# Units of 512 tokens in place of 256 in the feed-forward stage behind the recurrence

## The chip, the cores and the metric

The kernel runs on one core of a Trainium2 chip. The metric is the time of one execution on the device in microseconds (us), the median of several runs. Engines: PE multiplies matrices (PEld is its weight load), DVE, ACT and POOL work elementwise, SP issues the DMAs.

## The reference

A recurrence over 768 steps for 4 x 8 heads of 40 channels makes 3072 tokens of 320 values; two feed-forward layers with 1536 hidden units follow.

```python
for t in range(S):
    y[:, :, t] = einsum('bhd,bhde->bhe', rt, state)
    Sa = einsum('bhde,bhe->bhd', state, at)
    state = state * wt[:, :, None, :] - einsum('bhd,bhe->bhde', Sa, bt) + einsum('bhd,bhe->bhde', vt, kt)
x = y.transpose(0, 2, 1, 3).reshape(B * S, H * D)          # 3072 x 320
g = x @ w_gate;  x = (g * sigmoid(g) * (x @ w_val)) @ w_out      # layer 1
x = (sigmoid(x @ w_gate2) * (x @ w_val2)) @ w_out2               # layer 2
```

## The kernel before, in words

The recurrence works in 12 blocks of 64 time steps, which are 256 tokens each. Beside it the kernel already runs part of layer 1: block m's tokens become a tile x, which goes to memory (xd) too, and as many of the twelve slices of 128 hidden units as are loaded by then (w1) are applied to it. `used[m]` keeps that number: few slices for the early blocks, 11 for the last. The partial sums go to memory (xs[1]) by way of the tile "ob", which has one buffer (L1028, L1029).

Values are kept as float32r in a high and a low part, so a product takes several matmuls. One unit is one block with one slice: `gate` (L771) makes 8 matmuls of 256 columns into a gate bank and 8 into a value bank (L799); ACT takes the sigmoid (L803), DVE multiplies by the gate in layer 1 alone (L805) and by the value (L806), ACT rounds the high part (hh, L807), POOL makes the low part (hl, L808); `add` (L811) then makes 3 matmuls of 320 columns for each 128 tokens (L817) into the output banks.

From the end of the recurrence on, `stream` (L833) runs a list of jobs, one per block: in layer 1 the slices that the block still lacks, in layer 2 all twelve. A unit's output matmuls are issued after the gate matmuls of the next unit. `each` hooks run beside a unit: in layer 1 they load the part sums (L1075) and advance the preparation of layer 2's weights w2 by one step (`load_w`, L678: 36 steps, three a slice, 2 of 384 columns and 1 of 320, with four DVE instructions L701, L702, L706, L707 in each); in layer 2 they reduce w for a check of its range (L1101, L1105, L1106), whose result decides at the end whether a slow path runs. At a block's end its sums are added to the parts and stored (L1085, L1086), or in layer 2 copied and sent to the output (L1093, L1094). Layer 1 fetches x from xd (L1058); layer 2 reads xs[1] and splits it (L734). The framework's scheduler fixes the order on each engine at compile time and may bring loads and preparations forward.

Memory: pools lie on a stack. m_x (one x of 7168 bytes a partition) and m_h (g, hh, hl of 1024 bytes in two buffers each, ob of 1280) are opened first and serve both stages; then m_wa (w1[0] to w1[2]) and at_static; then, in the recurrence, at_work; when it is closed the new stage opens m_wb, m_y (part 2560, xin 3072, wt 1280, two buffers each), m_xq and m_tmp in at_work's place. Eight banks of PSUM: in the recurrence tp (2), zy, qu, pg, mm and two output banks; then two for transposes, two gate, two value and two output banks.

Of the kernel before, what the change touches and what calls it, by code (L numbers as in the profile page):

```python
# [18 lines left out]
P = 128  # L19
# [5 lines left out]
NWB = 2  # L25
# [644 lines left out]
class Ffn:  # L670
# [63 lines left out]
    def split_steps(self, xs):  # L734

        nc = self.nc
        x = self.new_x()
# [24 lines left out]
        yield x  # L762
# [5 lines left out]
    def sums(self, tag):  # L768
        return [self.po.tile([P, DM], F32, tag=f"{tag}{u}", name=f"{tag}{u}") for u in range(2)]

    def gate(self, x, w, silu):  # L771
# [3 lines left out]
        xh, xl = (x[:, 512 * i : 512 * i + 512].rearrange("p (k t) -> p k t", k=2) for i in range(2))  # L775
        t5 = x[:, 1024:1280]
        hd = x[:, 1536:], x[:, 1280:1536]
        if self.one_bank:
            pool, tag = self.pg[self.turn % len(self.pg)]
            gv = pool.tile([P, 2, 256], F32, tag=tag, name="gv")  # L780
            gv = [gv[:, 0], gv[:, 1]]
        else:
            gv = [self.pg.tile([P, 256], F32, tag=f"g{n}", name=f"g{n}") for n in range(2)]
        self.turn += 1
        for n in range(2):
            h = lambda k: wh[:, (3 * n + k) * P : (3 * n + k + 1) * P]
            l = lambda k: wl[:, (2 * n + k) * P : (2 * n + k + 1) * P]
            seq = [
                (h(0), xh[:, 0]),
                (h(1), xh[:, 1]),  # L790
                (l(0), xh[:, 0]),
                (l(1), xh[:, 1]),
                (h(2), t5),
                (h(0), xl[:, 0]),
                (h(1), xl[:, 1]),
                (wl[:, 4 * P : 5 * P], hd[n]),
            ]
            for e, (p, q) in enumerate(seq):
                nc.tensor.matmul(gv[n], lhsT=p, rhs=q, start=e == 0, stop=e == len(seq) - 1)  # L799
        g = self.h.tile([P, 256], F32, tag="g", name="g")  # L800
        hh = self.h.tile([P, 256], F32R, tag="hh", name="hh")
        hl = self.h.tile([P, 256], F32R, tag="hl", name="hl")
# [6 lines left out]
        return hh, hl  # L809
# [11 lines left out]
    def ffn(self, x, ws, silu, tag):  # L821

        ops, pend = self.sums(tag), None
        for f, w in enumerate(ws):
            h = self.gate(x, w, silu)
# [7 lines left out]
    def stream(self, jobs):  # L833
# [6 lines left out]
        for j, (ws, silu, tag, _, each, end) in enumerate(jobs):  # L840
# [3 lines left out]
            ops = self.sums(tag)  # L844
            for f, w in enumerate(ws):
# [11 lines left out]
                if f >= len(ws) - 4 and (nx := next(get, None)) is not None:  # L857
                    get = iter((nx,))
# [117 lines left out]
def rwkv_moe_kernel(ctx, tc, r, k, v, w, a, b, aw0, aw, aa, akb, av, avt, art, w1a, w2a, out):  # L976
# [11 lines left out]
    with ExitStack() as c1:  # L988
        pool = lambda n, b, **kw: c1.enter_context(tc.tile_pool(name=n, bufs=b, **kw))
        x_p, h_p = pool("m_x", 1), pool("m_h", 2)  # L990
# [6 lines left out]
        with ExitStack() as c2:  # L997
            pool2 = lambda n, b: c2.enter_context(tc.tile_pool(name=n, bufs=b, space=PSUM))
# [38 lines left out]
        with ExitStack() as c2:  # L1037
            pool2 = lambda n, b, **kw: c2.enter_context(tc.tile_pool(name=n, bufs=b, **kw))
            wb = pool2("m_wb", NWB)
            y_p, x_q = pool2("m_y", 2), pool2("m_xq", 1)  # L1040
            pt, pg, po = pool2("b_tp", 2, space=PSUM), pool2("b_pg", 2, space=PSUM), pool2("b_po", 1, space=PSUM)
# [4 lines left out]
            slots = [(wb, "w8")] * NWB + [(st, t) for t in spare_tags] + first + [(st, t) for t in tags]  # L1046
# [8 lines left out]
            def load_x(blk):  # L1055
                ffn.x = (x_q, x_p)[blk % 2]
                x = ffn.new_x()
                nc.sync.dma_start(out=x.bitcast(F32), in_=xd[blk])  # L1058
                yield x

            def split_x(blk):
                xin = y_p.tile([P, 2, DM + 64], F32, tag="xin", name="xin")
                src = xs[1][2 * blk : 2 * blk + 2].rearrange("u p e -> p u e")
                nc.sync.dma_start(out=xin[:, :, 0:DM], in_=src)
                nc.sync.dma_start(out=xin[:, :, DM:], in_=src[:, :, 256:DM])
                yield
                ffn.x = (x_q, x_p)[blk % 2]
                yield from ffn.split_steps([xin[:, 0], xin[:, 1]])
# [3 lines left out]
            def each1(blk, f):  # L1072
                if f == 0:
                    part = parts[blk] = y_p.tile([P, 2, DM], F32, tag="part", name="part")
                    nc.sync.dma_start(out=part, in_=xs[1][2 * blk : 2 * blk + 2].rearrange("u p e -> p u e"))  # L1075
                if 1 <= f <= 3:
                    next(ahead, None)
                if blk == NB - 1 and f == NF - 1 - used[blk]:
                    for _ in ahead:
                        pass  # L1080

            def end1(blk, ops):
                part = parts.pop(blk)
                for u in range(2):
                    nc.vector.tensor_tensor(out=part[:, u], in0=ops[u], in1=part[:, u], op=ALU.add)  # L1085
                    nc.sync.dma_start(out=xs[1][2 * blk + u], in_=part[:, u])  # L1086
# [3 lines left out]
            def end2(blk, ops):  # L1090
                ob = y_p.tile([P, 2, DM], F32, tag="part", name="ob")
                for u in range(2):
                    (nc.scalar.copy, nc.vector.tensor_copy)[u](out=ob[:, u], in_=ops[u])  # L1093
                    nc.sync.dma_start(out=out_rows(out, 2 * blk + u), in_=ob[:, u])  # L1094

            def check(blk, f):

                if f in (2, 6, 10):
                    if (n := 3 * blk + f // 4) < 2 * NB:
# [7 lines left out]
                if blk != NB - 2 or f != 8:  # L1107
# [15 lines left out]
            for blk in range(NB):  # L1123
                jobs.append((w1[used[blk] :], True, "po", load_x(blk), partial(each1, blk), partial(end1, blk)))
            for blk in range(NB):
                jobs.append((w2, False, "po", split_x(blk), partial(check, blk), partial(end2, blk)))
# [54 lines left out]
```

## Time and profile before

| what | value |
|---|---|
| median of 3 runs | 1341.2 us (1338.21 to 1343.47) |
| the profiled execution | 1342.04 us, span 1340.3 us |
| mean granted clock of PE | 0.93 |
| PE busy | 1228.5 us, 92% of the span |
| DVE, POOL, ACT busy | 798.8, 599.5, 584.6 us |

Busy shares are means over stages: the recurrence takes the first 690 us, the rest of layer 1 runs to about 920, layer 2 to the end. PE's matmuls are pipelined, so one of 283 ns can follow the other after less; distances between starts tell the pace.

### The profile page before, as it was taken

How to read it: one execution, taken by the hardware profiler on the slowest of the kernel's cores; microseconds unless marked ns; L12 is line 12 of the kernel's file. 1: busy time of each engine (PE TensorE's matmuls, PEld its weight loads, DVE VectorE, ACT ScalarE, POOL GpSimd, SP SyncE). 2: the span in 40 equal slices, each digit the busy share in tenths (PEclk: the TensorE clock that was granted, in tenths of full speed). 3: DMA queues.
4: the chain of work that ended last, by engine and by line, in shares of the span. 5: the costliest groups of instructions: out<-in, count | busy, mean ns of one | idle time of the engine just before them, and what ended most of it. 6: DMA issues, size and time to landing. Idle time of an engine off the chain costs nothing.

```text
span 1340.3 us, 32630 instructions
## 1 busy us (share of the span) xinstructions
PE 1228.5 (92%) x13197; PEld 1166.4 (87%) x13197; DVE 798.8 (60%) x1600; ACT 584.6 (44%) x1416; POOL 599.5 (45%) x798
## 2 busy tenths in 40 slices
PE   4556788799999999999899999999999999999996
PEld 4445777698899888888889999999999999999996
DVE  9778897976687677866879888833112221122111
ACT  5345446456655565545443444423333333333331
POOL 4278586432323322446766888722222222222221
PEclk7565689699999999989999999999999999999998
DMA  6733848645533454143356454221000000000000
GB/s 194 184 101 90 190 139 183 164 110 139 144 114 83 122 143 103 54 123 115 118 185 191 161 163 153 94 70 66 22 23 22 22 23 23 22 23 23 11 11 14
DMA packets 177202, 131.91 MB, mean 98 GB/s; under 512 B 123409, under 2 KB 155153, under 8 KB 176657
## 3 DMA queue, kind: packets, MB, share of 16 engines
q1 hardware_dynamic: 177040, 129.72, 34.8%
q8 instruction: 106, 1.74, 0.5%
q14 instruction: 56, 0.45, 0.1%
HBM read 96.14 MB, written 33.55 MB: 97 GB/s over the span
## 4 chain that ended last, share of the span: by engine, by line
PE 69%; DVE 16%; DMA 4%; issue 3%; ACT 3%; POOL 2%; SPq 2%; DVEq 0%; ACTq 0%; POOLq 0%
PE g L799 28%; PE po L817 16%; PE gv L799 7%; PE tp L312 3%; PE yps L586 3%; PE aps L560 3%; DVE pr L419 3%; PE kps L372 2%; DVE dt L702 2%; DVE part L425 2%; DVE dt L701 1%; PE ups L514 1%; PE qps L496 1%; DVE ds L706 1%; DVE ds L707 1%
## 5 line engine op out<-in xcount | busy, mean ns | idle before, releaser
L799 PE MATMUL g<-x,w 128*128 128x256 f32 x3552 | 494.8, 283 | 4.9 <-issue 3.0
L799 PEld LDWEIGHTS g<-x,w 128*128 128x128 f32 x3552 | 464.3, 190 | 6.3 <-issue 3.3
L808 POOL TENSOR_TENSOR hl<-g,hh 128x256 fp32r<-128x256 f32 x288 | 220.0, 765 | 474.0 <-ACT hh L807 418.7
L806 DVE TENSOR_TENSOR g<-g,g 128x256 f32<-128x256 f32 x222 | 93.8, 423 | 310.5 <-PE g L799 302.4
L807 ACT CAST hh<-g 128x256 fp32r<-128x256 f32 x288 | 117.0, 406 | 261.8 <-DVE g L806 239.2
L817 PE MATMUL po<-w,hh 128*128 128x320 f32 x1152 | 224.3, 311 | 2.3 <-ACT hh L807 1.8
L817 PEld LDWEIGHTS po<-w,hh 128*128 128x128 f32 x1152 | 175.5, 189 | 3.8 <-ACT hh L807 2.6
L799 PE MATMUL gv<-x,w 128*128 128x256 f32 x1056 | 153.8, 296 | 7.4 <-ACT x L751 5.5
L799 PEld LDWEIGHTS gv<-x,w 128*128 128x128 f32 x1056 | 137.1, 196 | 13.5 <-ACT x L751 8.2
L803 ACT ACTIVATE g<-g 128x256 f32<-128x256 f32 x222 | 84.8, 384 | 134.7 <-PE g L799 119.8
L817 PE MATMUL po<-w,hl 128*128 128x320 f32 x576 | 141.3, 316 | 0.6 <-POOL hl L808 0.6
L719 POOL TENSOR_TENSOR dt<-dt,w 128x384 f32<-128x384 f32 (+1 forms) x72 | 79.9, 1110 | 75.2 <-ACT w L717 42.1
L419 DVE TENSOR_TENSOR pr<-part,sn 128x4 f32<-128x4 f32 (+4 forms) x180 | 111.3, 619 | 3.7
L817 PEld LDWEIGHTS po<-w,hl 128*128 128x128 f32 x576 | 91.8, 190 | 2.7 <-POOL hl L808 1.8
L425 DVE TENSOR_REDUCE part<-pr 128x2 f32<-128x4 f32 (+4 forms) x180 | 88.8, 494 | 4.2
L372 PE MATMUL kps<-lq,kbt 104*128 104x128 f32 x384 | 65.6, 324 | 20.2 <-DVE lq L384 17.4
L372 PEld LDWEIGHTS kps<-lq,kbt 104*128 104x128 f32 x384 | 57.6, 229 | 24.7 <-issue 16.0
L384 DVE TENSOR_TENSOR lq<-kps,part 64x256 f32<-64x256 f32 x96 | 40.5, 422 | 64.6 <-ACT bn L382 62.7
L312 PE MATMUL tp<-ident,part 128*104 128x128 f32 x288 | 52.2, 311 | 16.1 <-DVE tkb L155 7.0
L334 POOL TENSOR_TENSOR tkb<-ld 128x320 f32<-128x320 f32 x44 | 47.7, 1105 | 37.0 <-DMA ld<-rd 21.8
L560 PE MATMUL aps<-rbd,ut 104*128 104x128 f32 x384 | 60.4, 302 | 3.9 <-DVE am L568 2.6
L717 ACT CAST w<-dt 128x384 fp32r<-128x384 f32 (+1 forms) x72 | 35.7, 495 | 53.2 <-DVE dt L702 50.8
(133 smaller groups left out, 1727.6 us busy)
## 6 DMA issues: line engine op xcount, KB each, us to landing
raw<-in_w_dram SPq DMA_DIRECT2D x48, 384.0 KB
xd<-x SPq DMA_DIRECT2D x12, 896.0 KB
x<-xd SPq DMA_DIRECT2D x12, 896.0 KB
raw<-in_w_dram SPq DMA_DIRECT2D x24, 320.0 KB
pn<-pd SPq DMA_DIRECT2D x46, 160.0 KB
ld<-in_a_kb_dram SPq DMA_DIRECT2D x22, 320.0 KB
ld<-rd SPq DMA_DIRECT2D x44, 160.0 KB
pd<-wp SPq DMA_DIRECT2D x12, 325.0 KB
```

What stands on the lines that cost most here:

```text
L312: nc.tensor.transpose(ps[0 : x.shape[1], n, :], x, ident)
L372: nc.tensor.matmul(kps[:, n].rearrange("p h t -> p (h t)"), lhsT=kbt[0:PW, n, :], rhs=lq[m % 3][0:PW, 4 * g4 + n].rearrange("p h t -> p (h ...
L419: nc.vector.tensor_tensor(out=o, in0=xs[:, 0:kk, None, 0:n].to_broadcast([P, kk, 2, n]), in1=sn[:, None, n : n + 2, 0:n].to_broadcast([P, ...
L425: nc.vector.tensor_reduce(out=xs[:, 0:kk, n : n + 2], in_=o, axis=AX.X, op=ALU.add)
L560: nc.tensor.matmul(aps[:, n, h2], lhsT=ut[0:PW, x, 2 * h2 : 2 * h2 + 2].rearrange("p u s -> p (u s)"), rhs=rbd[0:PW, x, h2].rearrange("p b ...
L719: sub(out=tf, in0=tf, in1=w.bitcast(F32), op=ALU.subtract)
L799: nc.tensor.matmul(gv[n], lhsT=p, rhs=q, start=e == 0, stop=e == len(seq) - 1)
L803: nc.scalar.activation(out=g, in_=gv[0], func=AF.Sigmoid)
L806: nc.vector.tensor_tensor(out=g, in0=gv[1], in1=g, op=ALU.mult)
L807: nc.scalar.copy(out=hh, in_=g)
L808: self.heng.tensor_tensor(out=hl, in0=g, in1=hh.bitcast(F32), op=ALU.subtract)
L817: self.nc.tensor.matmul(ops[u], lhsT=p[:, us], rhs=q, start=first and n == 0, stop=last and n == 2)
```

## The change

The jobs behind the recurrence take pairs of blocks, 512 tokens, so that a gate matmul has 512 columns. Gate and value have one bank of 512 values each instead of two of 256, and there are four output banks. Where the two blocks of a pair lack different slices of layer 1, the pair takes the slices that both lack and a job of its own does the rest for one block, with sums that go through memory once more. m_x and m_h are opened inside the recurrence's part and closed with it; the new stage opens m_y, m_xq (two x tiles of two blocks, 14336 bytes each) and m_hq (g, hh, hl of 2048 bytes, two buffers) and m_tmp; m_wb goes, and w2 starts in tiles of the recurrence. In layer 1 the hooks advance the weights by one step at units 1 to 6 of a job, all that is left in the last job, and x of the next job is asked for six units ahead instead of four.

```diff
-    def sums(self, tag):
-        return [self.po.tile([P, DM], F32, tag=f"{tag}{u}", name=f"{tag}{u}") for u in range(2)]
+    def sums(self, tag, n=2):
+        return [self.po.tile([P, DM], F32, tag=f"{tag}{u}", name=f"{tag}{u}") for u in range(n)]
...
     def gate(self, x, w, silu):
-        xh, xl = (x[:, 512 * i : 512 * i + 512].rearrange("p (k t) -> p k t", k=2) for i in range(2))
-        t5 = x[:, 1024:1280]
-        hd = x[:, 1536:], x[:, 1280:1536]
+        nt = x.shape[1]
+        part = lambda c: x[:, :, 256 * c : 256 * c + 256]
+        hd = part(6), part(5)
...
-            gv = [self.pg.tile([P, 256], F32, tag=f"g{n}", name=f"g{n}") for n in range(2)]
+            gv = [self.pg.tile([P, nt, 256], F32, tag=f"g{n}", name=f"g{n}") for n in range(2)]
...
-        for u in range(2):
+        for u in range(len(ops)):
             us = slice(u * P, u * P + P)
...
-                if f >= len(ws) - 4 and (nx := next(get, None)) is not None:
+                if f >= len(ws) - 6 and (nx := next(get, None)) is not None:
...
-        x_p, h_p = pool("m_x", 1), pool("m_h", 2)
         wa, st = pool("m_wa", NFA - 2), pool("at_static", 1)
...
         with ExitStack() as c2:
+            x_p, h_p = (c2.enter_context(tc.tile_pool(name=n, bufs=b)) for n, b in (("m_x", 1), ("m_h", 2)))
...
-            wb = pool2("m_wb", NWB)
-            y_p, x_q = pool2("m_y", 2), pool2("m_xq", 1)
-            pt, pg, po = pool2("b_tp", 2, space=PSUM), pool2("b_pg", 2, space=PSUM), pool2("b_po", 1, space=PSUM)
+            y_p, x_p, h_p = pool2("m_y", 2), pool2("m_xq", 2), pool2("m_hq", 2)
+            pt, pg, po = pool2("b_tp", 2, space=PSUM), pool2("b_pg", 1, space=PSUM), pool2("b_po", 1, space=PSUM)
...
-            slots = [(wb, "w8")] * NWB + [(st, t) for t in spare_tags] + first + [(st, t) for t in tags]
+            slots = [(st, t) for t in spare_tags] + first + [(st, t) for t in tags]
...
+            def new_x(n):
+                return x_p.tile([P, n, XW], F32R, tag="x", name="x")
+
+            def load_x(bs):
+                x = new_x(len(bs))
+                for i, blk in enumerate(bs):
+                    nc.sync.dma_start(out=x[:, i].bitcast(F32), in_=xd[blk])
                 yield x
...
+            def each1(bs, at, final, f):
+                if f == at:
+                    for blk in bs:
+                        part = parts[blk] = y_p.tile([P, 2, DM], F32, tag="part", name="part")
+                        nc.sync.dma_start(out=part, in_=xs[1][2 * blk : 2 * blk + 2].rearrange("u p e -> p u e"))
+                if final:
                     for _ in ahead:
                         pass
+                elif 1 <= f <= 6:
+                    next(ahead, None)
+
+            def end1(bs, ops):
+                for i, blk in enumerate(bs):
+                    part = parts.pop(blk)
+                    for u in range(2):
+                        nc.vector.tensor_tensor(out=part[:, u], in0=ops[2 * i + u], in1=part[:, u], op=ALU.add)
+                        nc.sync.dma_start(out=xs[1][2 * blk + u], in_=part[:, u])
...
+            def end2(bs, ops):
+                for i, blk in enumerate(bs):
+                    ob = y_p.tile([P, 2, DM], F32, tag="part", name="ob")
+                    for u in range(2):
+                        (nc.scalar.copy, nc.vector.tensor_copy)[u](out=ob[:, u], in_=ops[2 * i + u])
+                        nc.sync.dma_start(out=out_rows(out, 2 * blk + u), in_=ob[:, u])
...
+            left = []
+            for blk in range(0, NB, 2):
+                lo, hi = sorted(used[blk : blk + 2])
+                if hi < NF:
+                    left.append(((blk, blk + 1), w1[hi:]))
+                if lo < hi:
+                    left.append(((blk + (used[blk] > used[blk + 1]),), w1[lo:hi]))
+            for i, (bs, ws) in enumerate(left):
+                jobs.append((ws, True, len(bs), load_x(bs), partial(each1, bs, min(2, len(ws) - 1), i == len(left) - 1), partial(end1, bs)))
+            for j in range(NB // 2):
+                bs = 2 * j, 2 * j + 1
+                jobs.append((w2, False, 2, split_x(bs), partial(check, j), partial(end2, bs)))
```

## Rows read from the trace of the kernel before

**Rows 1.** Busy us of each engine by stretches, granted clock, DMA share, GB/s:

```profile
core 0: us, PE busy (x) PEld busy (x) DVE busy (x) ACT busy (x) POOL busy (x), PEclk, DMA share, GB/s
800.00:840.00 40.00, 39.26 (x306) 38.69 (x305) 35.48 (x63) 17.68 (x45) 33.20 (x44) 1.00 0.49 158
1000.00:1040.00 40.00, 40.00 (x319) 40.00 (x318) 7.65 (x18) 13.12 (x34) 10.96 (x16) 1.00 0.07 19
```

**Rows 2.** Timeline of PE in layer 2: start, length from first start to last end:

```profile
1004.03 1.83 PE L799 MATMUL g<-x,w 128*128 128x256 f32 x14
...
1006.82 1.83 PE L799 MATMUL g<-x,w 128*128 128x256 f32 x14
```

**Rows 3.** The page's costliest groups: busy, mean ns, idle before:

```profile
L799 PE MATMUL g<-x,w 128*128 128x256 f32 x3552 | 494.8, 283 | 4.9 <-issue 3.0
```

**Rows 4.** Output matmuls (L817) between the blocks' end adds, twelve stretches:

```profile
698.10:730.80 32.70, 11.64 (x60) 9.01 (x60) 1.00 0.59 178
...
920.00:924.00 4.00, 1.25 (x6) 0.91 (x6) 1.00 0.24 86
```

**Rows 5.** Timeline of PE where the recurrence ends:

```profile
690.34 0.56 PE L817 MATMUL po<-w,hl 128*128 128x320 f32 x2
693.95 4.38 PE L799 MATMUL g<-x,w 128*128 128x256 f32 x22 [3.05 <-issue]
```

**Rows 6.** Timeline of DVE at that place:

```profile
690.86 0.47 DVE L1105 TENSOR_REDUCE wacc<-wt 128x1 f32<-128x320 f32 x1
...
693.43 0.41 DVE L806 TENSOR_TENSOR g<-gv,g 128x256 f32<-128x256 f32 x1
```

**Rows 7.** Timeline of the DMA issues (SPq) there:

```profile
678.56 0.33 SPq L1058 DMA_DIRECT2D x<-xd  x1
...
689.24 0.33 SPq L1058 DMA_DIRECT2D x<-xd  x1
...
700.37 0.34 SPq L1029 DMA_DIRECT2D xs<-ob  x1
```

**Rows 8.** Groups by form from 790 us on: busy, mean ns, idle before:

```profile
L808 POOL TENSOR_TENSOR hl<-g,hh 128x256 fp32r<-128x256 f32 x191 | 142.9, 749 | 324.2 <-ACT hh L807 323.3
...
L807 ACT CAST hh<-g 128x256 fp32r<-128x256 f32 x190 | 77.2, 406 | 191.2 <-DVE g L806 171.2 <-PE po L817 17.2 <-PE g L799 2.6
...
L752 DVE TENSOR_TENSOR x<-xtp,x 128x512 fp32r<-128x512 f32 x12 | 8.3, 690 | 5.8 <-ACT x L751 5.8
...
L751 ACT CAST x<-xtp 128x512 fp32r<-128x512 f32 x12 | 7.0, 587 | 14.2 <-PE xtp L745 12.9 <-PE g L799 1.4
```

**Rows 9.** Timeline of ACT, the last two copies of the recurrence's sums:

```profile
699.92 0.43 ACT L1028 COPY ob<-po 128x320 f32<-128x320 f32 x1
...
702.24 0.43 ACT L1028 COPY ob<-po 128x320 f32<-128x320 f32 x1
```

**Rows 10.** DMA traffic from 689.3 to 694.3, the second x load:

```profile
DMA packets 591, 1.49 MB, mean 297 GB/s; under 512 B 58, under 2 KB 424, under 8 KB 591
```

**Rows 11.** Busy us of the engines in the stretch behind the idle time:

```profile
694.00:698.00 4.00, 4.00 (x21) 4.00 (x22) 3.88 (x9) 1.65 (x4) 3.64 (x5) 0.57 0.52 164
```

**Rows 12.** Timeline of DVE in layer 1:

```profile
756.76 0.42 DVE L805 TENSOR_TENSOR g<-g,g 128x256 f32<-128x256 f32 x1
...
759.60 0.42 DVE L806 TENSOR_TENSOR g<-g,g 128x256 f32<-128x256 f32 x1
```

**Rows 13.** Waits of PE from 694 to 915: us in total, times, longest:

```profile
PE g L799 <- DVE g L806: 1.1, 2, 0.8
PE g L799 <- DVE g L805: 0.7, 2, 0.6
```

**Rows 14.** DMA issues around a block's end in layer 1:

```profile
871.85 0.92 SPq L1086 DMA_DIRECT2D xs<-part  x2
874.23 0.39 SPq L1075 DMA_DIRECT2D part<-xs  x1
```

**Rows 15.** DMA issues at the end of the kernel:

```profile
1329.13 1.12 SPq L1094 DMA_DIRECT2D out_dram<-ob  x2
```

**Rows 16.** Busy us, clock, DMA share and GB/s at the end:

```profile
1331.00:1339.00 8.00, 0.00 (x0) 0.00 (x0) 0.00 (x0) 0.00 (x0) 0.00 (x0) 0.61 0.14 46
```

More of the change, by code (lines that the diff above doesn't have):

```diff
@@ L24 @@
 NFA = 5
-NWB = 2
 DM = H * D
@@ L732, in split, with split_steps @@
         return x
-    def split_steps(self, xs):
+    def split_steps(self, xs, x=None):
         nc = self.nc
-        x = self.new_x()
+        x = self.new_x() if x is None else x
         lo, hi = slice(0, 64), slice(64, 128)
@@ L788, in gate @@
             seq = [
[L789 to L795, printed above, removed]
+                (h(0), part(0)),
+                (h(1), part(1)),
+                (l(0), part(0)),
+                (l(1), part(1)),
+                (h(2), part(4)),
+                (h(0), part(2)),
+                (h(1), part(3)),
                 (wl[:, 4 * P : 5 * P], hd[n]),
@@ L799, in gate @@
                 nc.tensor.matmul(gv[n], lhsT=p, rhs=q, start=e == 0, stop=e == len(seq) - 1)
-        g = self.h.tile([P, 256], F32, tag="g", name="g")
-        hh = self.h.tile([P, 256], F32R, tag="hh", name="hh")
-        hl = self.h.tile([P, 256], F32R, tag="hl", name="hl")
+        g = self.h.tile([P, nt, 256], F32, tag="g", name="g")
+        hh = self.h.tile([P, nt, 256], F32R, tag="hh", name="hh")
+        hl = self.h.tile([P, nt, 256], F32R, tag="hl", name="hl")
         nc.scalar.activation(out=g, in_=gv[0], func=AF.Sigmoid)
@@ L808, in gate @@
         self.heng.tensor_tensor(out=hl, in0=g, in1=hh.bitcast(F32), op=ALU.subtract)
-        return hh, hl
+        return [t.rearrange("p n t -> p (n t)") for t in (hh, hl)]
     def add(self, ops, w, h, first, last):
         (hh, hl), oh, ol = h, w[0][:, 6 * P :], w[1][:, 5 * P :]
-        for u in range(2):
+        for u in range(len(ops)):
             us = slice(u * P, u * P + P)
@@ L824, in ffn @@
         for f, w in enumerate(ws):
-            h = self.gate(x, w, silu)
+            h = self.gate(x[:, None], w, silu)
             if pend is not None:
@@ L839, in stream @@
         get = jobs[0][3]
-        for j, (ws, silu, tag, _, each, end) in enumerate(jobs):
+        for j, (ws, silu, nt, _, each, end) in enumerate(jobs):
             for x in get:
@@ L843, in stream @@
             get = iter(()) if j + 1 == len(jobs) else jobs[j + 1][3]
-            ops = self.sums(tag)
+            ops = self.sums("po", 2 * nt)
             for f, w in enumerate(ws):
@@ L1053, in rwkv_moe_kernel @@
             ahead = load_w2()
[L1055 to L1058, printed above, removed]
-                yield x
[L1061 to L1065, printed above, removed]
+            def new_x(n):
+                return x_p.tile([P, n, XW], F32R, tag="x", name="x")
@@ new lines, in load_x, with split_x @@
+            def load_x(bs):
+                x = new_x(len(bs))
+                for i, blk in enumerate(bs):
+                    nc.sync.dma_start(out=x[:, i].bitcast(F32), in_=xd[blk])
+                yield x
+            def split_x(bs):
+                xins = []
+                for blk in bs:
+                    xin = y_p.tile([P, 2, DM + 64], F32, tag="xin", name="xin")
+                    src = xs[1][2 * blk : 2 * blk + 2].rearrange("u p e -> p u e")
+                    nc.sync.dma_start(out=xin[:, :, 0:DM], in_=src)
+                    nc.sync.dma_start(out=xin[:, :, DM:], in_=src[:, :, 256:DM])
+                    xins.append(xin)
@@ L1066, in split_x @@
                 yield
-                ffn.x = (x_q, x_p)[blk % 2]
-                yield from ffn.split_steps([xin[:, 0], xin[:, 1]])
+                x = new_x(len(bs))
+                for i, xin in enumerate(xins):
+                    for y in ffn.split_steps([xin[:, 0], xin[:, 1]], x[:, i]):
+                        yield None if y is None or i < len(bs) - 1 else x
             parts = {}
[L1072 to L1078, printed above, removed]
+            def each1(bs, at, final, f):
+                if f == at:
+                    for blk in bs:
+                        part = parts[blk] = y_p.tile([P, 2, DM], F32, tag="part", name="part")
+                        nc.sync.dma_start(out=part, in_=xs[1][2 * blk : 2 * blk + 2].rearrange("u p e -> p u e"))
+                if final:
@@ L1079, in each1 @@
                     for _ in ahead:
                         pass
[L1082 to L1086, printed above, removed]
-            wf = aw.rearrange("p (u x) -> (p u) x", u=8)
[L1090 to L1094, printed above, removed]
@@ new lines, in rwkv_moe_kernel, with check @@
+            wf = aw.rearrange("p (u x) -> (p u) x", u=8)
+            def end2(bs, ops):
[4 more added lines that the diff above has]
+                        nc.sync.dma_start(out=out_rows(out, 2 * blk + u), in_=ob[:, u])
+            def check(j, f):
+                if f % 2:
+                    if (n := 6 * j + f // 2) < 2 * NB:
```

11 lines of the change are left out of this document (2 added, 9 removed).

## The prediction

> **What bounds the kernel now.** I read the busy times by stretches first, then single units on the timeline, then the counts, last the two seams: the start of the stage that changes and the end of the kernel. In that stage PE is busy 39.26 of 40 us at 800 and 40.00 of 40 at 1000, at a granted clock of 1.00, while DVE falls from 35 to 8 [rows 1]. So PE bounds the part that the change rewrites, and its units follow each other without a gap: the same place of the pattern comes at 1004.03 and 1006.82, a unit each 2.79 us [rows 2]. Fourteen gate matmuls of 256 columns span 1.83 us and the last takes 0.28, so they start every 1.55/13 = 119.2 ns; then 6 output matmuls of 320 columns have 2.79 - 16 x 0.1192 = 0.88 us, 147 ns each. At 2.4 GHz (clock 1.00) the columns alone are 106.7 and 133.3 ns: both widths carry about 13 ns on top.
>
> How many units there are: 3552 gate matmuls (tile g) are 222 units of 16 [rows 3]; layer 2 has 12 x 12 = 144, so 78 of layer 1 are left after the recurrence. The output matmuls between the blocks' end adds (6 a unit; the first stretch also holds 6 of the recurrence's last unit) are 60 in the first of twelve stretches and 6 in the last [rows 4]; counted through they give 9, 9, seven times 7, 6, 4, 1. The new list of jobs follows: pairs (0,1) x9, (2,3), (4,5), (6,7) x7, (8,9) x6; block 8 alone x1; (10,11) x1; block 10 alone x3. That is 37 wide and 4 narrow units, and 72 wide ones in layer 2: 109 wide units.
>
> **Part 1, the width.** Sixteen matmuls of 512 columns replace 32 of 256. If the extra 13 ns belong to the matmul, one costs 213.3 + 12.7 = 226 ns against 2 x 119.2 = 238.4: 12.4 ns saved, x 16 x 109 = 21.6 us. The trace has no 512-column matmul. Bounds: nothing, if the extra grows with the columns, and 25.1 x 16 x 109 = 44 us, if it vanishes. The two widths at hand carry 12.5 and 13.7 ns, so I take the fixed one: **-21.6**. The output matmuls stay as many and as wide.
> The Trainium skill (TensorE: Matmul & The Clock Gate, "Back-to-back issue gap") gives N/2.4 + 2.5 ns a matmul, by which merging saves 2.5 ns, an estimated 4.4 us in all; it speaks against the change, but it would put 256 columns at 109 and 320 at 136 ns, and the trace has 119 and 147. The 131 ns that the section gives for a stream of N=512 is already under the trace's 147 at 320.
>
> **Part 2, the start.** PE's last recurrence matmul starts before 690.9, and the first gate matmul of the new stage comes at 693.95 after 3.05 us of idleness [rows 5]. What ends just then is L806 at 693.43 + 0.41, the read of the recurrence's last value bank [rows 6], though the gate bank, by the order of the pools, lies where the recurrence's L586 wrote and not that unit: a new pool waits for everything in the pools whose memory it takes over. Now x: before, its first tile lay over the recurrence's work pool and its load went out at 678.56, the second, over the shared x pool, at 689.24 [rows 7]. After, the pools m_x and m_h move into the recurrence's own stack: 7168 + 7424 = 14592 bytes a partition, ahead of at_work. The new stage puts m_y there first (2 x 6912 = 13824 bytes), then m_xq. So the first x tile begins 768 bytes inside m_h, where "ob" is its last tile, and m_y lies over it as well. The x loads thus wait for the last ob to be stored. That chain, from rows: L806 ends about 693.0 (the reductions ahead of it, two in 0.8 us, came with the early loads that now also wait); hh 0.41, hl 0.75 [rows 8], the last output matmuls and hand-overs 0.85: 695.0. The first ob copy 0.43; the second starts 2.32 after the first (699.92, 702.24 [rows 9]) because ob has one buffer and its store must land; its own store goes out 0.46 later and lands 1.87 after that (issue 700.37 [rows 7] to copy 702.24). That is 699.9. Then two blocks of 896 KB, 1.835 MB, at the 297 GB/s of the second load before [rows 10], 6.2 us, and an estimated 1 us until the first bytes move: PE starts at about 707 instead of 694. The wait also lets the clock drop: before, 694 to 698 ran at 0.57 after 3 us of idleness [rows 11], and the first 22 gate matmuls took 4.38 us [rows 5] where 119 ns each make 2.8, so half speed cost 1.6 us; now perhaps 2.5. The 6 last output matmuls (0.9) fall into the idle time. **+13**; -2 if x is not held up, +18 if other loads get in between, or the stores take twice as long.
>
> **Part 3, single gate banks beside the weight preparation.** A bank must be free when the next unit's gate group starts: 8 x 0.226 + 12 x 0.147 = 3.6 us after the gate group's end (before, two banks left 4.6). With 512 columns the sigmoid takes about 0.59 and the product 0.69, judged by the 512-wide L751 and L752 [rows 8]; with 0.15 of hand-over 1.4 us, so 2.0 us are to spare. In layer 2 that covers all. In layer 1 the same DVE queue prepares w2 (L701, L702, L706, L707, in 36 steps), and is 35 of 40 us busy [rows 1]. Between 756.76 + 0.34 and 759.60 all four of a step of 320 columns stand between L805 and L806 of one unit, 2.5 us [rows 12]; at the 384 that two steps of three have, an estimated 3.0. Such a unit would now make PE wait up to 1.0 us. Some 30 steps fall among 37 wide units; if a fifth of that us is lost in each wide unit, 7 us, less the 1.8 that PE lost to L805 and L806 before [rows 13]: **+5**, bounds 0 and +18 (half a us in each).
>
> **Part 4, the ragged end of layer 1.** Block 8 and block 10 are each done twice, so their sums go to memory and come back: store, landing, load. The x tile of (10,11) can load only after the last gate of (8,9), and PE has 1.8 + 1.9 + 1.8 = 5.4 us of other work against about 7.3 for the load: 2 us. The part of block 11 takes the buffer of block 8's second part, so it waits for that store (2.4 us from the first L1086 to the next L1075, which waits for them [rows 14]) and then for its own load of an estimated 2.7, some 5.6 us against PE's 3.7; L1085 then blocks DVE, and the silu product behind it holds the next gate bank: 1 to 1.5 us. Wide jobs advance one weight step at each of units 1 to 6, 29 steps; seven are left for the last job, beside its silu products; their w2 tiles are needed some 50 us later. **+3.5**, bounds 0 and +9.
>
> **Part 5, the tail.** The last value matmul is followed by L806, L807, L808, output matmuls, copies, out DMAs. Product +0.27, cast +0.18, hl from 0.75 to an estimated 1.5 for twice the columns [rows 8]: +1.2; six of the output matmuls that stood ahead of the last value matmul now stand behind it, -0.9. The two out DMAs go out from 1329.13 on [rows 15], and from 1331 to 1339 memory moves only 46 GB/s, the 16 DMA engines 0.14 busy [rows 16]: two engines' worth, where the x loads had 297. So 320 KB take 7.1 us. Now both blocks of the last pair end together: four DMAs, 7.1 us more. **+7.4**, bounds +2 (other engines serve the second pair) and +9.
> The Trainium skill (DMA: Bandwidth & Descriptors, "Why a DMA increments its semaphore by 16 and not by 1") says that the slowest dimension sets the number of engines, always the lowest-numbered: here 2 (dimension c), the same two for all four. The trace agrees in the share (two of 16 are 0.125); that a second pair queues behind the first, no run here shows yet.
>
> **Costed at nothing.** The four copies of a layer-2 pair (two on ACT, two on DVE) must clear the output banks before the next pair's first output matmuls; a whole gate unit, 3.6 us, runs in between, and they take about 1 us; uncovered they would cost that 5 times. Without the two m_wb slots w2[0] goes into a tile of the recurrence and w2[10], w2[11] into those of w1[5], w1[6], which are read until block 8's narrow job; ten layer-2 units, 54 us, pass before they are needed, against some 25 us for six steps at the pace of L1 before; if they came later, PE would wait by that much, once. The split of x for the next pair starts six units ahead; its six transposes a block are the same as before. The minimum and maximum over w (L1105, L1106) move from the start to wherever DVE has room, with the last layer-1 units as the limit that hurts (part 3). The end adds of a pair are four instead of two, 2 us of DVE, under the 3.6 us of the next gate unit.
>
> **Sum.** -21.6 + 13 + 5 + 3.5 + 7.4 = +7.3. The profiled execution takes 1342.0 us (span 1340.3), 0.8 above the runs' median of 1341.2; so 1349.3, and I say 1349 us for the median. A measurement of this kernel tells about 0.5% from no change: 1334.5 to 1347.9.
>
> **Rivals.**
> A, the sum above, chance 0.55. Its own spread is 5 to 6 us, so six tenths of it is slower, the rest the same.
> B, x is not held up: the loads go out near 679 as before. Then part 2 is -2 instead of +13: 1334, the other side or the edge of it; every us earlier than 707 comes off the sum, so from a start before 699.7 on the kernel is no slower than before. For it: before, the loads were early. Against: the byte sums. Chance 0.15, half faster.
> C, DVE becomes the bound in layer 1: L805, L806, a weight step and, 24 times in all, two reductions are 4.4 to 5.3 us of a 5.4 us unit, and any slip makes PE wait: part 3 at +18 to +25, 1362 to 1369. Against: DVE was as full before and PE waited little [rows 13]. Chance 0.13.
> D, the width buys nothing, since the extra follows the columns: 1371. Here the skill's gap formula belongs. Chance 0.06.
> E, the extra vanishes at 512: 1327. Chance 0.06. Something else 0.05.
> Slower by over 0.5%: 0.33 + 0.13 + 0.06 + 0.01 = 0.53; within: 0.22 + 0.08 + 0.03 = 0.33; faster: 0.07 + 0.06 + 0.01 = 0.14. Range 1333 to 1365: A, most of B, the near half of C; A alone 1341 to 1358.
>
> **What would show it.** Right: 512-column matmuls 226 ns apart, a layer-2 pair of blocks in 65 to 66 us; x loads issued behind the last store of ob, a PE gap of 10 us or more before the first wide matmul, at half clock behind it; out DMAs working for 14 us at the end. Wrong: x issued near 679, PE waiting over 0.5 us in every layer-1 unit, the four out DMAs landing together.

## The result and the profile after

The changed kernel takes 1356.5 us (median of 4 runs, 1355.6 to 1360.6) against 1342.0 us (median of 4 runs beside it): a ratio of 1.0118, 95% interval 1.0088 to 1.0149. It is slower by 14.5 us, where the prediction said +7.3 us for the profiled execution and 1349 us for the median. The profiled execution of the changed kernel is the longest of the four, 1360.6 us with a span of 1358.9 us; before it was 1342.0 with 1340.3. So the two traces differ by 18.6 us. In layer 2 the last 72 x 16 gate matmuls are counted back from the end, and this gives four pieces:

| piece (us) | before | after | difference |
|---|---|---|---|
| start of the trace to the first gate matmul of the new stage | 693.95 | 710.21 | +16.3 |
| from there to the first gate matmul of layer 2 | 223.3 | 227.4 | +4.2 |
| from there to the last gate matmul | 408.9 | 399.0 | -9.9 |
| from there to the end | 14.2 | 22.2 | +8.0 |

Of the +16.3, 1.6 is no part of the change: in this execution the recurrence ran later (the first copy of the sums, tile ob, of its last block but one starts at 657.39 after and at 655.77 before).

**The start.** The timelines of PE and of the DMA issues (SPq) of the changed kernel where the recurrence ends (start, length, what; idle time before it in brackets):

```profile
693.71 0.86 PE L816 MATMUL po<-w,hh 128*128 128x320 f32 x4 [0.61 <-ACT hh L806]
695.94 0.74 PE L816 MATMUL po<-w,hl 128*128 128x320 f32 x2 [1.37 <-POOL hl L807]
710.21 4.17 PE L798 MATMUL g<-x,w 128*128 128x512 f32 x11 [13.53 <-DVE dt L701]
```
```profile
696.90 2.67 SPq L1028 DMA_DIRECT2D xs<-ob  x2
699.66 0.38 SPq L688 DMA_DIRECT2D raw<-in_w_dram  x1
701.13 0.80 SPq L1059 DMA_DIRECT2D x<-xd  x2
701.98 1.05 SPq L1082 DMA_DIRECT2D part<-xs  x2
703.07 2.19 SPq L1059 DMA_DIRECT2D x<-xd  x2
```

The x loads, issued at 678.56 before [rows 7], now go out at 701.13, behind the second store of ob. PE has finished the recurrence's sums and idles 13.53 us. The releaser that the row names, a weight conversion on DVE, only ended at about that moment; the experiment below shows that x was awaited. Busy us of the engines by stretches, granted clock, DMA share and GB/s:

```profile
698.00:702.00 4.00, 0.00 (x0) 0.00 (x0) 1.67 (x3) 1.28 (x3) 2.26 (x4) 0.50 0.44 138
702.00:706.00 4.00, 0.00 (x0) 0.00 (x0) 2.56 (x5) 0.91 (x2) 2.96 (x5) 0.50 0.87 299
706.00:710.00 4.00, 0.00 (x0) 0.00 (x0) 2.72 (x5) 1.34 (x3) 2.56 (x4) 0.50 1.01 380
710.00:714.00 4.00, 3.79 (x11) 3.05 (x12) 1.29 (x3) 0.80 (x3) 2.47 (x3) 0.60 1.00 413
```

The DMA engines are full from 706 us on, and the clock, at 0.50 (1.2 GHz) while PE idles, is still 0.60 in the stretch after it: the first 11 wide matmuls take 4.17 us, where 10 starts of 0.233 and one length of 0.39 make 2.7.

**Layer 2.** Two units of 512 tokens that hold no transposes, on PE's timeline:

```profile
1027.51 3.89 PE L798 MATMUL g<-x,w 128*128 128x512 f32 x16
1031.24 1.34 PE L816 MATMUL po<-w,hh 128*128 128x320 f32 x8
1032.42 0.75 PE L816 MATMUL po<-w,hl 128*128 128x320 f32 x4
1033.01 3.89 PE L798 MATMUL g<-x,w 128*128 128x512 f32 x16
```

A unit takes 1033.01 - 1027.51 = 5.50 us against 2 x 2.79 = 5.58 for the same tokens before [rows 2]; over all of layer 2 the middle unit of the kernel before takes 2.80, so 5.60. With 12 output matmuls at 147 ns, 16 wide ones have 3.74 us: 233 ns each, not the predicted 226. So 0.08 to 0.10 us is saved in a unit, 9 to 11 us in 109.

**Layer 1.** The vector engine's timeline through one unit of layer 1, and what PE waited for from 714 to 938 us (us in total, times, longest):

```profile
733.63 0.67 DVE L805 TENSOR_TENSOR g<-g,g 128x512 f32<-128x512 f32 x1
734.23 0.34 DVE L700 TENSOR_SCALAR dt<-dt 128x384 int32<-128x384 int32 x1
734.49 0.47 DVE L1114 TENSOR_REDUCE wacc<-wt 128x1 f32<-128x320 f32 x1
734.89 0.47 DVE L1115 TENSOR_REDUCE wacc<-wt 128x1 f32<-128x320 f32 x1
735.28 1.46 DVE L701 SCALAR_TENSOR_TENSOR dt<-raw,dt 128x384 int32<-128x384 int32 x1
736.67 0.47 DVE L1114 TENSOR_REDUCE wacc<-wt 128x1 f32<-128x320 f32 x1
737.06 0.47 DVE L1115 TENSOR_REDUCE wacc<-wt 128x1 f32<-128x320 f32 x1
737.46 0.34 DVE L705 TENSOR_SCALAR ds<-dt 128x384 int32<-128x384 int32 x1
737.72 0.68 DVE L804 TENSOR_TENSOR g<-g,g 128x512 f32<-128x512 f32 x1
```
```profile
PE g L798 <- DVE g L804: 2.8, 6, 1.3
PE g L798 <- DVE g L805: 0.9, 4, 0.2
PE xtp L744 <- DMA xin<-xs: 0.7, 1, 0.7
PE po L816 <- DVE part L1093: 0.2, 1, 0.2
```

Between the value product of one gate and the silu product of the next stand four range reductions of the weights w and three conversion steps, 3.4 us without a gap. The gate bank comes free only with that silu product, so PE waits for it (L804). In the kernel before, 8 of the 48 reductions ran ahead of the first gate and 40 in layer 1 (to 735.7); with two gate and two value banks PE waited little [rows 13].

**The end.** The out DMAs of the changed kernel, and the engines, clock, DMA share and GB/s behind them:

```profile
1340.87 6.49 SPq L1103 DMA_DIRECT2D out_dram<-ob  x4
```
```profile
1342.00:1358.00 16.00, 0.00 (x0) 0.00 (x0) 0.00 (x0) 0.00 (x0) 0.00 (x0) 0.58 0.14 46
```

Four stores instead of two [rows 15], at the same 0.14 and 46 GB/s as before [rows 16], for twice as long: 1358.92 - 1340.87 = 18.05 us from the first issue to the end, against 1340.32 - 1329.13 = 11.19.

### The profile page after: what moved, and what is told of

Read it like the earlier page. It is cut to its first block, busy times and chain, and to the rows that moved or that the text cites. A ratio compares the mean times of both kernels' runs of the same rounds, so it can differ in the third digit from the quotient of the medians.

```text
span 1358.9 us, 28352 instructions
## 1 busy us (share of the span) xinstructions
PE 1228.8 (90%) x11453; PEld 1082.3 (80%) x11453; DVE 773.8 (57%) x1458; ACT 548.0 (40%) x1198; POOL 579.3 (43%) x689
## 4 chain that ended last, share of the span: by engine, by line
PE 67%; DVE 16%; DMA 6%; ACT 3%; issue 3%; SPq 2%; POOL 2%; DVEq 0%; ACTq 0%; POOLq 0%
PE g L798 27%; PE po L816 16%; PE gv L798 8%; PE tp L311 3%; PE aps L559 3%; PE yps L585 3%; DVE pr L418 3%; PE kps L371 2%; DVE dt L701 2%; PE qps L495 2%; PE ups L513 2%; DVE part L424 1%; DMA wq<-in_a_w_dram 1%; DVE dt L700 1%; DVE ds L706 1%
## 5 line engine op out<-in xcount | busy, mean ns | idle before, releaser
L798 PE MATMUL g<-x,w 128*128 128x512 f32 (+1 forms) x1808 | 440.4, 394 | 17.4 <-DVE dt L701 13.5
L807 POOL TENSOR_TENSOR hl<-g,hh 128x512 fp32r<-128x512 f32 (+1 forms) x179 | 197.7, 1105 | 491.5 <-ACT hh L806 435.4
L798 PEld LDWEIGHTS g<-x,w 128*128 128x128 f32 x1808 | 330.1, 188 | 91.2 <-ACT dt L696 13.9
L805 DVE TENSOR_TENSOR g<-g,g 128x512 f32<-128x512 f32 (+1 forms) x113 | 76.9, 680 | 316.0 <-PE g L798 315.2
L816 PE MATMUL po<-w,hh 128*128 128x320 f32 x1152 | 209.8, 312 | 1.4 <-ACT hh L806 1.0
L806 ACT CAST hh<-g 128x512 fp32r<-128x512 f32 (+1 forms) x179 | 96.0, 536 | 250.1 <-DVE g L805 249.5
L816 PEld LDWEIGHTS po<-w,hh 128*128 128x128 f32 x1152 | 181.6, 188 | 12.4 <-ACT hh L806 1.4
L798 PEld LDWEIGHTS gv<-x,w 128*128 128x128 f32 x1056 | 139.1, 199 | 12.5 <-ACT x L750 8.5
L802 ACT ACTIVATE g<-g 128x512 f32<-128x512 f32 (+1 forms) x113 | 66.5, 589 | 202.4 <-PE g L798 198.7
L816 PE MATMUL po<-w,hl 128*128 128x320 f32 x576 | 125.6, 316 | 1.9 <-POOL hl L807 1.8
L371 PE MATMUL kps<-lq,kbt 104*128 104x128 f32 x384 | 65.2, 322 | 22.6 <-DVE lq L383 18.6
L311 PE MATMUL tp<-ident,part 128*104 128x128 f32 x288 | 52.4, 313 | 16.9 <-DVE tkb L154 7.0
```

The lines of the kernel that those rows point to most:

```text
L311: nc.tensor.transpose(ps[0 : x.shape[1], n, :], x, ident)
L371: nc.tensor.matmul(kps[:, n].rearrange("p h t -> p (h t)"), lhsT=kbt[0:PW, n, :], rhs=lq[m % 3][0:PW, 4 * g4 + n].rearrange("p h t -> p (h ...
L802: nc.scalar.activation(out=g, in_=gv[0], func=AF.Sigmoid)
L805: nc.vector.tensor_tensor(out=g, in0=gv[1], in1=g, op=ALU.mult)
L806: nc.scalar.copy(out=hh, in_=g)
L807: self.heng.tensor_tensor(out=hl, in0=g, in1=hh.bitcast(F32), op=ALU.subtract)
```

## The experiments

The theory: three losses that have nothing to do with each other (x held up at the start, DVE's products late for single banks in layer 1, the stores at the end), against a gain by the width that is smaller than predicted. The rival for each was that something else holds PE at that place, so that the undone part would bring nothing.

**x_clear_of_ob**: the pools of the new stage in another order.

```diff
-y_p, x_p, h_p = pool2("m_y", 2), pool2("m_xq", 2), pool2("m_hq", 2)
+y_p, tmp, x_p, h_p = pool2("m_y", 2), pool2("m_tmp", 1), pool2("m_xq", 2), pool2("m_hq", 2)
...
-tmp = pool2("m_tmp", 1)
```


> The pools after the recurrence are laid out in another order (the conversion's temporaries second, then the x tiles and the h tiles), so that the first x tile no longer begins inside the region of the recurrence's output staging tile; nothing else is changed. My theory (the x loads were held by the last store of that tile): the x loads are issued near 679 to 690 us as before the change, the first wide gate starts at 694 to 697 us instead of 710.2, and the median falls by 13 to 17 us, to 1340 to 1344 us. Rival (the banks, the weights or the vector engine at the end of the recurrence hold the first wide gate anyway): it starts at 705 us or later and the median stays above 1350 us.

Measured: 1343.8 us (12 runs), ratio 1.0005 (0.9993 to 1.0018), 12.7 us under the changed kernel and within the 1340 to 1344 us expected. The DMA issues, and PE's first wide gate, which comes earlier than the 694 to 697 expected:

```profile
681.95 2.08 SPq L1058 DMA_DIRECT2D x<-xd  x4
688.93 0.33 SPq L688 DMA_DIRECT2D raw<-in_w_dram  x1
695.76 0.34 SPq L1028 DMA_DIRECT2D xs<-ob  x1
```
```profile
690.05 3.98 PE L798 MATMUL g<-x,w 128*128 128x512 f32 x16 [0.28 <-DMA x<-xd]
```

With 3072 bytes between m_y and the x tiles, the loads go out 19 us earlier, PE starts 20 us earlier, at full clock, and the recurrence's last sums run between the wide gates. From the first gate to layer 2 it takes 230.4 us instead of 227.4; eight output matmuls of the recurrence, 1.2 us, now lie inside this stretch. What follows: the wait at the start is x behind ob, as predicted, and it costs 12.7 us.

**x_contiguous**: in layer 2 x is laid out [part, chunk, token], so that the moving operand is 512 columns in one piece.

```diff
-part = lambda c: x[:, :, 256 * c : 256 * c + 256]
+part = lambda c: x[:, c]
...
-xh, xl, t5, hd = x[:, 0:512], x[:, 512:1024], x[:, 1024:1280], x[:, 1280:1536]
+xh, xl, t5, hd = x7[:, 0:2], x7[:, 2:4], x7[:, 4], x7[:, 5]
```


> In layer 2 alone the x tile is laid out by part and then by chunk, so that the moving operand of a wide gate matmul is 512 columns in one piece instead of two pieces of 256; layer 1 keeps the two pieces. Theory A (the second piece costs the 5 to 6 ns by which a wide matmul missed the forecast): the spacing of layer-2 gate matmuls falls from 232 to 226 or 227 ns, layer 2 from 399.0 to 392 or 393 us, and the median to about 1350 us. Theory B (what a matmul costs over its columns grows with the columns: 12.5 ns at 256, 13.7 at 320, about 18 at 512): the spacing stays at 231 to 232 ns in both layers, and the median at 1356 us.

Measured: 1355.8 us (6 runs), ratio 1.0112 (1.0094 to 1.0129). Layer 2 takes 399.04 us in both traces, and the median spacing of its gate matmuls is 232 ns, against 233 with two pieces. Theory A falls. What a matmul costs over its columns is not fixed: 12.5 ns at 256 columns, 13.7 at 320, and about 19 to 20 at 512.

**halves**: the changed kernel with every wide gate matmul issued as two of 256 columns.

```diff
-for e, (p, q) in enumerate(seq):
-    nc.tensor.matmul(gv[n], lhsT=p, rhs=q, ...)
+for i, (e, (p, q)) in [(i, y) for i in range(nt) for y in enumerate(seq)]:
+    nc.tensor.matmul(gv[n][:, i : i + 1], lhsT=p, rhs=q[:, i : i + 1], ...)
```


> Units, banks, pools and every other operation stay those of the changed kernel, but each gate matmul of 512 columns is issued as two of 256 (one accumulation group of eight after the other in the same bank). This measures what the width alone is worth. By the traced spacings (2 x 119.2 against 232 ns, 1744 matmuls) it costs 10 to 13 us, median 1367 to 1369 us. By my forecast (226 ns) it costs 21 to 22 us, 1378 us. If the width bought nothing, the median stays within 3 us of 1356.5 us.

Measured: 1364.8 us (5 runs), ratio 1.0174 (1.0157 to 1.0191), 8.3 us over the changed kernel. A unit without transposes on PE:

```profile
1000.90 3.99 PE L798 MATMUL g<-x,w 128*128 128x256 f32 x32
...
1006.50 3.99 PE L798 MATMUL g<-x,w 128*128 128x256 f32 x32
```

5.60 us for what the wide matmuls do in 5.50, which is 0.10 in a unit and 11 us in 109. By the medians the width is worth 8.3 us, by the units 9 to 11: at or a little under the 10 to 13 expected from the median spacings and far under the 21.6 predicted.

**out_split**: each output store as two of 64 rows.

```diff
-nc.sync.dma_start(out=out_rows(out, 2 * blk + u), in_=ob[:, u])
+rows = out_rows(out, 2 * blk + u)
+for b2 in range(2):
+    nc.sync.dma_start(out=rows[b2], in_=ob[64 * b2 : 64 * b2 + 64, u])
```


> Each output store of 128 rows is issued as two of 64 rows, nothing else is changed. My theory (the four last stores go over two DMA engines, 0.14 of the DMA's time and 46 GB/s in the last 16 us): they spread over the 16 engines, the time from the last gate matmul to the end falls from 22.2 to 12 to 15 us, and the median to 1346 to 1350 us. Rival (what sets the tail is the chain of the last products and copies and the fixed time of a store): it falls by less than 2 us.

Measured: 1353.2 us (6 runs), ratio 1.0077 (1.006 to 1.0094), 3.3 us under the changed kernel. The issues, and the stretch behind them:

```profile
1340.63 6.20 SPq L1105 DMA_DIRECT2D out_dram<-ob  x8
```
```profile
1342.00:1350.00 8.00, 0.00 (x0) 0.00 (x0) 0.00 (x0) 0.00 (x0) 0.00 (x0) 0.66 0.37 84
```

The DMA share rises from 0.14 to 0.37, and in the trace the last piece falls from 22.2 to 14.9 us. The tail came as expected; the median, which should have come to 1346 to 1350 us, did not: it fell by 3.3 us. The next run gives 5.9 for the same edit. Single executions differ by some us before the new stage begins (the first ob copy of the recurrence's last block but one starts between 651.7 and 657.4 us in the traces so far), so the 7.3 us of the trace is the better measure of the stores and the medians of what they are worth; the gap of 1.4 to 4 us is not explained.

**clear_split**: the edits of x_clear_of_ob and out_split together.

> The pool order of x_clear_of_ob and the split stores of out_split together. If the two losses are separate, the median is that of x_clear_of_ob less the 7.3 us that the last stretch lost in the trace of out_split (22.2 to 14.9 us): 1336 to 1338 us, 4 to 6 us under the kernel before. Rival (the medians of out_split, 3.3 us under the changed kernel, show what splitting is worth, and the rest of the 7.3 us comes back elsewhere): 1340 to 1341 us.

Measured: 1337.9 us (12 runs), ratio 0.9974 (0.9961 to 0.9986). That is 5.9 us under x_clear_of_ob. The two losses are separate, and without them the changed kernel is 0.3% faster than the kernel before as it stood; with its own stores split (before_split below, 1338.2 us) that kernel is as fast.

**clear_split_bank**: in addition one bank for the transposes and two for the value product.

```diff
-pt, pg, po = pool2("b_tp", 2, space=PSUM), ...
+pt, pg, po = pool2("b_tp", 1, space=PSUM), ...
...
-gv = [self.pg.tile([P, nt, 256], F32, tag=f"g{n}", name=f"g{n}") for n in range(2)]
+gv = [self.pg.tile([P, nt, 256], F32, tag=f"g{n}", name=f"g{n}", bufs=1 + n) for n in range(2)]
```


> clear_split, with one bank fewer for the transposes and a second bank for the value product. Theory (in layer 1 the tensor engine waits 12 us in all, 10 us more than before, because with single banks the next gate can't start until the vector engine has made its two products): the excess in layer 1 falls from about 12 to under 4 us, the median to 1327 to 1331 us. Rival (the vector engine is simply full there, so that a bank moves the wait and doesn't take it away): the excess stays above 9 us and the median within 2 us of clear_split. A second rival: the single bank of the transposes adds waits in layer 2, where there are nearly none now.

Measured: 1333.3 us (6 runs), ratio 0.9943 (0.9925 to 0.9961), 4.6 us under clear_split. Layer 1 falls from 229.9 to 222.9 us, layer 2 rises from 399.1 to 402.5 and the end from 15.0 to 16.9. The excess of PE's spacings in layer 1 (each start that comes over 0.27 us after the one before it, less 0.232) falls from 11.6 to 6.9 us, not to 4, and the idle time before a gate that is put down to the value product (L805), 0.8 us in clear_split, is gone. So the bank does part of it. The lengths of the pieces show this only roughly: the scheduler set another order, by which 12 output matmuls and 8 transposes passed from layer 1 to layer 2. In layer 2 the excess rises from 1.3 to 3.2 us; the second rival is borne out in that direction, but whether the one transpose bank or the order does it the runs don't tell.

**clear_no_range**: x_clear_of_ob without the 48 range reductions.

```diff
-nc.vector.tensor_reduce(out=acc[:, 0, n : n + 1], in_=wt, axis=AX.X, op=ALU.max)
-nc.vector.tensor_reduce(out=acc[:, 1, n : n + 1], in_=wt, axis=AX.X, op=ALU.min)
+if n == 0:
+    nc.vector.memset(acc, 0.5)
```


> x_clear_of_ob without the 48 reductions on the vector engine that find the range of the decay weights (their loads stay, the range is a constant): this part of the computation is left out. Theory (the waits in layer 1 are products of the vector engine that stand behind these reductions and the weight conversions): the excess in layer 1 falls from 12 us to 3 to 6 us, the median from 1343.8 to 1335 to 1340 us. Rival (the conversions alone do it): the excess stays above 10 us and the median above 1342 us.

Measured: 1335.3 us (6 runs), ratio 0.9949 (0.9929 to 0.9969), 8.5 us under x_clear_of_ob. The same 40 us of layer 1, first x_clear_of_ob and then without the reductions (busy us and counts of PE, PEld, DVE, ACT, POOL):

```profile
720.00:760.00 40.00, 36.52 (x176) 29.48 (x175) 38.80 (x76) 12.95 (x26) 24.73 (x30) 1.00 0.60 196
```
```profile
720.00:760.00 40.00, 40.00 (x207) 34.71 (x206) 33.26 (x50) 15.10 (x29) 31.94 (x36) 1.00 0.74 241
```

DVE falls from 38.80 to 33.26 of 40 us, and PE issues 207 matmuls instead of 176. What PE waited for in layer 1, x_clear_of_ob and then without the reductions:

```profile
PE g L798 <- DVE g L804: 5.1, 9, 1.0
PE po L816 <- DVE part L1092: 1.2, 2, 1.0
PE g L798 <- DMA x<-xd: 1.0, 2, 0.7
PE g L798 <- DVE g L805: 0.7, 2, 0.5
```
```profile
PE g L798 <- DMA x<-xd: 1.4, 2, 1.1
PE po L816 <- DVE part L1092: 1.2, 2, 1.0
```

The waits for both products are gone, and the excess in layer 1 falls from 12.2 to 2.5 us, further than the 3 to 6 expected: the reductions made the products late, the conversions alone do not. What is left are the waits for x and for the end adds (L1092).

**clear_split_late**: clear_split with the reductions held back until layer 1 has ended, by two tiles that share their buffers.

```diff
+held = []
+for n in range(2):
+    d = y_p.tile([P, DM], F32, tag="wt", name="held")
+    nc.gpsimd.memset(d[:, 0:1], 0.0)
+    held.append(d)
...
+if bs is left[-1][0]:
+    for d in held:
+        nc.vector.tensor_tensor(out=d[:, 0:1], in0=part[:, 1, 0:1], in1=d[:, 0:1], op=ALU.max)
```


> clear_split with the 48 range reductions held back until layer 1 has ended (their two buffers are also written by the last unit of layer 1, so that their loads and they themselves come in layer 2, where the vector engine is 10 to 20 percent busy); everything is computed. If the reductions in layer 1 are what makes its products late, the 8.5 us that clear_no_range gained come back without leaving anything out: layer 1 takes 220 to 223 us, layer 2 stays within 1 us of 399.0, median 1328 to 1331 us. Rival (in layer 2 they hold up the value product there as they did in layer 1): layer 2 takes 404 us or more and the median stays above 1334 us.

Measured: 1330.8 us (6 runs), ratio 0.9928 (0.9914 to 0.9942), 7.1 us under clear_split, with the whole computation done. Layer 1 takes 220.4 us as expected. Layer 2 takes 402.4 instead of 399.1, more than the 1 us allowed for: the rival's direction at less than its size (its excess rises from 1.3 to 4.7 us). This is the lowest median of all, though its interval overlaps those of clear_split_bank and before_split_late.

**before_split** and **before_split_late**: the same edits on the kernel before.

> The kernel before with its output stores split into two of 64 rows. My theory: its two last stores (14.2 us from the last gate matmul to the end) lose 3 to 5 us, median 1337 to 1339 us: the changed kernel's tail is longer because it has twice as many such stores behind the last product. Rival (they overlap the other end work): less than 1 us.

> The same two edits on the kernel before: split stores, and the 48 range reductions held back until layer 1 has ended. With two gate banks and two value banks the kernel before waited only 1.7 to 2.5 us in layer 1, so holding the reductions back gains at most 2 us over before_split: median 1336 to 1338 us. If it gains 5 us or more, the reductions cost the kernel before as much as the changed one, and single banks are not what made them dear. Against clear_split_late it also shows what the wide units are worth once start, layer 1 and end are equal: by the trace of halves 8 to 9 us.

Measured: 1338.2 us (12 runs), ratio 0.9969 (0.9953 to 0.9985), and 1333.6 us (5 runs), ratio 0.9935 (0.9922 to 0.9948). The first was as expected by the median, 3.6 us lower; in the trace the end falls by 2.5 us, from 14.2 to 11.7. The second missed: holding the reductions back gained 4.6 us where at most 2 were expected. One place shows on PE, where the recurrence ends, first before_split and then before_split_late:

```profile
692.39 4.36 PE L799 MATMUL g<-x,w 128*128 128x256 f32 x22 [3.05 <-issue]
```
```profile
693.85 2.86 PE L799 MATMUL g<-x,w 128*128 128x256 f32 x22 [0.47 <-issue]
```

The reductions ran at the recurrence's end already, ahead of the read of its last value bank [rows 6]. Without them the idle time of [rows 5] falls from 3.05 to 0.47 us, and the matmuls behind it take 2.86 us instead of 4.36, at a clock that did not fall. That is not the whole account. Counted from the ob copy above, the first gate comes only 2.3 us earlier, since the recurrence's last matmuls end later. Layer 1 is 4.0 us shorter (222.2 to 218.2): the 1.5 us of clock, and PE's waits there, whose excess falls from 1.7 to 0.1 us. Layer 2, where the reductions now are, is 2.4 us longer (408.9 to 411.3).

## Why the prediction was right, and where its size was off

The likeliest case, a slower kernel by the sum of five parts, came true. The sum was 7.2 us too low for the median (+14.5 against +7.3), and 9.7 too low for the traces, once the 1.6 us of the later recurrence are taken off. Three of the losses were foreseen at the right place; that layer 1 came out in sum was in part luck, since the term that it grew by had been put at nothing.

**Part 1, the width: the term that was mis-sized.** -21.6 predicted; 8.3 us by the medians of halves, 9 to 11 by the units. The step that failed is "I take the fixed one": the 12.5 and 13.7 ns at 256 and 320 columns looked fixed, but were the first two points of a rise, 233 - 213.3 = 20 ns at 512. The truth lies nearer to the rival D (25 ns, no gain) than to the fixed 12.7. Two pieces in the operand are not the cause (x_contiguous); what is, no run here shows. This error of 11 to 13 us is larger than the whole error of the sum.
By the gap formula of the Trainium skill (TensorE: Matmul & The Clock Gate, "Back-to-back issue gap") 512 columns would take an estimated 216 ns; the section gives it for an isolated matmul, which the prediction left out, and 131 ns for a stream. The trace has 233, above both. The saving that the formula gave, an estimated 4.4 us, missed the measured one by 4 to 7 us.

**Part 2, the start: right.** +13 predicted, 14.7 in the trace (16.3 less 1.6). Counted in the same way from the ob copy, the traces of halves, out_split and x_contiguous, whose start is that of the changed kernel, give 11.3, 12.4 and 12.7. The 12.7 us of x_clear_of_ob agree, but that is against a repaired kernel, whose first gate comes earlier (690.05) than that of the kernel before (693.95). The chain came in the order written, each step 1 to 3 us later: first ob copy at 696.45 (695.0 predicted), the second 2.33 behind it, x issued at 701.13 (699.9), first wide matmul at 710.21 (about 707), half clock behind it. Loads left out of the chain share the DMA engines with the first pair's x: a raw load issued at 699.66, the part loads at 701.98 and the next pair's x from 703.07 on.

**Parts 3 and 4, layer 1: right in sum, with another owner.** +5 and +3.5 predicted. Measured: +4.2 for layer 1, which holds 37 wide units at -0.08 to -0.10, so +7 to +8 beside the width. The half clock at its beginning is no part of this, since it costs both kernels about 1.5 us (4.38 us where 2.8 would do [rows 5], 4.17 where 2.7 would). Without it the excess of PE's spacings, measured as above, grows from 2.5 to 8.3 us, and 12 transposes for layer 2 now lie in this piece, 1.3 us at 0.11 each. In the traces of x_contiguous and out_split, whose layer 1 has the same work, it takes 229.5 and 229.9 us, 2 to 2.5 more than in this execution.

The waits have two places. In the stretch of the range reductions the excess is 6.4 to 6.6 us in these three traces; the waits for the last blocks' x and end adds, which part 4 had put at +3.5, cost 1.0, 2.6 and 3.6. So the ragged end was foreseen with its mechanism, and in size in two traces of three. Single banks are a part of the first place, as clear_split_bank shows, but the work that makes the products late there is not the conversion step that part 3 costed. It is the 24 pairs of range reductions, costed at nothing because they would go "wherever DVE has room". They went into the first 57 us of layer 1 (716.7 to 767.6), where DVE had none. This is rival C's mechanism at a third of its size. Removing the reductions takes 10 us off layer 1 (230.4 to 220.2 us, clear_no_range).

**Part 5, the tail: right.** +1.2 to the first out DMA and +7.1 behind it predicted; measured from the last gate matmul's start to the first out DMA 4.17 (1340.87 - 1336.70) against 3.03, so +1.1, and behind it 18.05 - 11.19 = +6.9. Eighteen output matmuls and the 12 transposes fewer lie in the piece of layer 2 in the table, 2.6 and 1.3 us of its -9.9: twelve of the output matmuls now stand behind the last gate matmul (the prediction's -0.9 counts six), six in the idle time at the start. The rule of the Trainium skill (DMA: Bandwidth & Descriptors, "Why a DMA increments its semaphore by 16 and not by 1") that was left open in the prediction agrees: two more stores take the same 0.14 for longer, and with the dimension of two taken out of the store the share rises to 0.37. That dimension is b, not c: `out_rows` fixes c by an index.

**What was costed at nothing and stayed so.** In layer 2 the changed kernel's spacings hold 1.3 us of excess in 399; copies and w2's places cost nothing to speak of. The split of x costs 0.7 us, once, in layer 1 (PE's wait for xin above).

With both stores and reductions repaired in each, wide units (1330.8) and narrow ones (1333.6) can't be told apart: their ratios to the kernel before overlap. In those two traces layer 2 is 8.8 us shorter with wide units (3.9 of it the output matmuls and transposes that lie elsewhere), layer 1 is 2.2 us longer and the end 3.6 us longer.

## What to carry to other kernels

A tile in a new pool can have to wait for what last used the bytes under it, so when pools move, work out the byte ranges: 768 bytes of overlap cost 12.7 us here, and moving one pool ahead of two others gave them back. (Whether a tile waits for the tiles under it or for everything in the old pool, no run here tells.) Work that "fills gaps" must be followed to the gap it lands in, because a scheduler that moves it up can set it ahead of the products that a bank waits for. Extrapolating a cost per instruction from two nearby sizes to twice the size needs both its fixed and its growing reading kept in the sum.

## What the runs showed of the hardware that was not expected

At a granted clock of 1.00 the time of a matmul with a new weight tile each time, over its columns, grew from 12.5 ns (256) and 13.7 (320) to about 20 (512), the same with the operand in one piece or two. And a releaser in a row can be one that only ended at the right moment: the 13.53 us before the first wide matmul are put down to a DVE conversion, and went when the x load went out earlier.
